# One decode step: the last row of wo in two column halves, the output in two PSUM banks, the tail of w_out on 12 lanes

## The chip, the cores and the metric

The kernel runs on one core of a Trainium2 chip. The core has a matrix engine (TensorE, PE in the profile, with its weight loads as PEld), a vector engine (VectorE, DVE), a scalar engine (ScalarE, ACT), GpSimd (POOL) and a sequencer that issues most of the DMAs (SyncE, SP), and 16 DMA engines that move data between device memory (HBM) and on-chip memory (SBUF). [...]

The metric is device time in microseconds (us) for one execution of the whole program. Three runs of the kernel before gave 661.06, 661.14 and 661.30 us; the median is 661.14.

## The reference

One token for each of 4 sequences is normalized (LayerNorm, D = 640) and goes through two branches in parallel, whose results are added to the input:

```python
xn = _layernorm(x)
return x + _A_ref(xn, k_cache, v_cache, wq, wo) + _B_ref(xn, w_in, w_sp, b_sp, w_out)

# A: attention over a cache, 32 heads of 128, 4096 positions, batch 4, bf16
q = (x @ wq) split into heads
scores = einsum('bhqd,bhkd->bhqk', q, k) * 128 ** -0.5
o = einsum('bhqk,bhkd->bhqd', softmax(scores), v)
return o (as rows of 4096) @ wo                  # wo: 4096 x 640

# B: gated MLP
z = gelu(einsum('bsd,df->bsf', x, w_in))         # w_in: 640 x 1728
z1, z2 = z[..., :864], layernorm(z[..., 864:])
g = w_sp * z2 + b_sp                             # 1 x 1 spatial weight
return einsum('bsf,fd->bsd', z1 * g, w_out)      # w_out: 864 x 640
```

K and V together are 268 MB of bf16, and each element is used once.

## The kernel before, in words

**Tiles.** The 32 heads are taken in four groups of eight. One step `i` of the main loop (16 in all) does one group of heads for one sequence; its K tile and its V tile are 8 MB each, 128 partitions by 64 KB, and each is loaded by one DMA. K has two slots in SBUF; V has one. wq first sits in a K slot, w_in and w_out first sit in the V slot (`w_sb`, lines 106 to 126), and wo takes the V slot at the end.

**Start.** SP issues w_out's first 768 rows (line 109), wq (114), w_in (121), the last 96 rows of w_out (line 123, four DMAs), and then the first K tile. These last 96 rows lie on `TL` = 16 lanes (partitions) with `TK` = 6 rows each, and each of the four DMAs fills 4 of the lanes (`TE`), every fourth one. The query projection (line 271) computes 4096 columns in two halves in two PSUM tiles of pool `ps_pv`; ACT copies each half (line 278), PE transposes it. The second K tile is issued when wq has been used.

**gMLP.** Branch B runs between the query projection and the loop (`gmlp`, lines 309 to 421). For the last 96 rows, `TK` small matmuls (line 408) gather the activations of every `TK`-th column on `TL` lanes (`ye_ps`, copied to `yE`). Then `NFC` = 12 calls of `add_out` add everything to the output: six on 128 lanes, six on 16 lanes. The first V tile may only be issued (line 145) when these matmuls have read w_sb.

**Loop.** DVE multiplies the K tile by the query in place (449), folds it in half (463); PE sums by matmuls with an identity (475), DVE finishes the row sums (486). Then maximum, exponential (542), the weights spread to each head's own lanes (553), and 64 matmuls per tile with V (`weighted`, 568) into one PSUM tile `pv`. ACT copies `pv` to `e` (`take`, 578) and PE picks each head's own rows out of `e` into `o_ps` (`diag`, 591). The order of PE, DVE, ACT and SP in the loop is the order in which the code is written.

**wo.** After the last step but one has used its V tile, SP issues wo (`load_wo`, line 154) into the V slot: the first half of the heads (`g` = 0) in one DMA, the second (`g` = 1) in three, rows 0 to 10, 11 to 14 and 15 of each partition (`WO_CUTS`). The last V tile is loaded before it, into a K slot.

**End.** After the last V tile: 64 matmuls, copy, `diag`, normalization and spreading (619, 628), turning (643), and the projection `group_proj` with 16 rows of four matmuls each (`add_out`, line 216), one for each quarter of the 640 columns. A quarter `q` lies in PSUM on partitions 32q to 32q + 3, all four in one bank, the tile `out_ps`. The four matmuls of row 15 stop the accumulation. Then ACT copies the first two quarters to `res` and DVE the last two (735), and each half is stored by a DMA of its own, the first from ACT's queue and the second from SP's (739).

Of the kernel before, what the change touches and what calls it, by code (L numbers as in the profile page):

```python
# [9 lines left out]
FP32 = mybir.dt.float32  # L10
# [7 lines left out]
def kernel(  # L18
# [14 lines left out]
    nc = tc.nc  # L33
    P = nc.NUM_PARTITIONS
    Bsz, Sq, D = A_x.shape
    _, H, S, Dh = A_k_cache.shape
    HD = A_wq.shape[1]
    F = B_w_in.shape[1]
    Fh = F // 2
# [18 lines left out]
    GW = P // CG  # L58
    ROWS = HT * Bsz
    NG = 2  # L60
    HP = HG // NG
    WH = NG * HT
    WL = P // WH
    WJ = WH * Dh // P
    WW = 2
    WR = NG * ROWS
    NFF = Fh // P
    TL = 16
    TK = (Fh - NFF * P) // TL
    TE = 4  # L70
    NFC = NFF + TK
    F0 = NFF * P
    TF = TL * TK
    NZ = NFF + 1
    assert F0 + TF == Fh and TF <= P
    NQ = 4
    NO = D // NQ
# [8 lines left out]
    pmp = ctx.enter_context(tc.tile_pool(name="pmp", bufs=1))  # L86
    PSUM = bass.MemoryType.PSUM
    ps_s = ctx.enter_context(tc.tile_pool(name="ps_s", bufs=1, space=PSUM))
    ps_pv = ctx.enter_context(tc.tile_pool(name="ps_pv", bufs=2, space=PSUM))
    ps_m = ctx.enter_context(tc.tile_pool(name="ps_m", bufs=2, space=PSUM))  # L90
    ps_o = ctx.enter_context(tc.tile_pool(name="ps_o", bufs=1, space=PSUM))
    ps_out = ctx.enter_context(tc.tile_pool(name="ps_out", bufs=1, space=PSUM))
# [4 lines left out]
    def v_slot(name):  # L97
        return vp.tile([P, SLOT], BF16, tag="v", name=name)
# [9 lines left out]
    w_out_sb = w_sb[:, DC * F : DC * F + NFC * D].rearrange("p (k n) -> p k n", k=NFC)  # L108
    nc.sync.dma_start(
        out=w_out_sb[:, 0:NFF, :], in_=B_w_out[0 : NFF * P].rearrange("(p k) n -> p k n", k=NFF)  # L110
# [10 lines left out]
    nc.sync.dma_start(out=w_in_sb, in_=B_w_in.rearrange("(p c) n -> p c n", c=DC))  # L121
    for l in range(TL // TE):
        nc.sync.dma_start(
            out=w_out_sb[:TL, NFF:NFC, :].rearrange("(e l) k n -> e l (k n)", e=TE)[:, l],
            in_=B_w_out[F0:Fh].rearrange("(e l k) n -> e l (k n)", e=TE, k=TK)[:, l],
        )

    def kv_view(cache, i):
# [8 lines left out]
    def load_k(i):  # L137
        t = k_slot("k_nat")
        nc.sync.dma_start(out=t[:], in_=kv_view(A_k_cache, i))
        k_tiles[i] = t[:].rearrange("p (c d) -> p c d", d=Dh)  # L140

    def load_v(i, t):
        cuts = V_CUTS if i == NT - 1 else (0, NC)
        for c0, c1 in zip(cuts, cuts[1:]):
            nc.sync.dma_start(
                out=t[:, c0 * Dh : c1 * Dh], in_=kv_view(A_v_cache, i)[:, c0 * Dh : c1 * Dh]
            )
        v_tiles[i] = t[:].rearrange("p (c d) -> p c d", d=Dh)

    wo_v = A_wo.rearrange("(g p j) n -> g p j n", p=P, j=WJ)  # L150
    wo_t = []
    WO_CUTS = ((0, WJ), (0, 11, 15, WJ))

    def load_wo():
        t = v_slot("wo")[:, 0 : HP * WJ * D].rearrange("p (g j n) -> p g j n", g=HP, n=D)
        wo_t.append(t)
        for g in range(HP):
            for j0, j1 in zip(WO_CUTS[g], WO_CUTS[g][1:]):
                nc.sync.dma_start(out=t[:, g, j0:j1, :], in_=wo_v[g][:, j0:j1, :])

    load_k(0)

# [19 lines left out]
    for i in range(NSTAT):  # L182
# [5 lines left out]
        out=rstd[:], in_=mv[:, 1:2], func=ACT.Sqrt, bias=eps_tile[:Bsz], scale=1.0  # L188
# [3 lines left out]
        out=xn_bf,  # L192
# [9 lines left out]
    for c in range(DC):  # L202
        nc.tensor.transpose(
            out=xnT_ps[:, c, :], in_=xn_v[:, c, :], identity=ident[:Bsz, :Bsz]
# [3 lines left out]
        out=xnT_r[:], in_=xnT_ps[:, :, :, None].to_broadcast([P, DC, Bsz, REP])  # L208
    )
    xnT = xnT_r[:, :, :, 0]  # L210

    out_ps = ps_out.tile([P, NO], FP32)

    def add_out(lhsT, rhs, start=False, stop=False):
        for q in range(NQ):
            nc.tensor.matmul(  # L216
                out=out_ps[GW * q : GW * q + lhsT.shape[1], :],
                lhsT=lhsT,
                rhs=rhs[:, q * NO : (q + 1) * NO],
                start=start,  # L220
                stop=stop,
            )
# [6 lines left out]
        out=own[:], in_=ident_f[:].rearrange("p (h l) -> p h l", h=HT), axis=AX.X, op=ALU.add  # L229
# [4 lines left out]
        out=pick[:, :, GW - HT : GW],  # L234
        in_=ident_f[:].rearrange("p (j h c) -> p c h j", c=CB, h=HT),
# [5 lines left out]
        out=row_head_f[:],  # L241
        in_=ident_f[:WR, :WR].rearrange("p (g b h) -> p g h b", g=NG, h=HT),
# [5 lines left out]
        out=row_head[:],  # L248
        in_=row_head_f[:].rearrange("p g h -> p (g h)")[:, :, None].to_broadcast([WR, WH, WL]),
# [3 lines left out]
        out=row_batch_f[:],  # L253
        in_=ident_f[:WR, :WR].rearrange("p (g b h) -> p b g h", g=NG, h=HT),
# [12 lines left out]
    for t in range(2):  # L267
        for c in range(DC):
            for j in range(CG):
                n = CG * t + j  # L270
                nc.tensor.matmul(  # L271
                    out=q_ps[t][GW * j : GW * (j + 1), :],
                    lhsT=xnT_r[:, c].rearrange("p b r -> p (b r)"),
# [5 lines left out]
    for t in range(2):  # L279
        qT_ps = ps_m.tile([P, HQ, CG, Bsz, REP], BF16, tag="m", name="qT_ps")  # L280
        for n in range(HQ):
            nc.tensor.transpose(  # L282
                out=qT_ps[:, n].rearrange("p j b r -> p (j b r)"),
                in_=q_rows[:, t, n * Dh : (n + 1) * Dh],
# [3 lines left out]
            out=qT[:, CG * HQ * t : CG * HQ * (t + 1), :].rearrange(  # L288
                "p (j n) b -> p n j b", n=HQ
            ),  # L290
            in_=qT_ps[:, :, :, :, 0],
# [17 lines left out]
    def gmlp():  # L309
# [95 lines left out]
        nc.vector.tensor_tensor(out=yT[:], in0=gz[:, 0, :, :], in1=sq, op=ALU.mult)  # L405
        ye_ps = ps_m.tile([TL, TK, Bsz], FP32, tag="m", name="ye_ps")
        for k in range(TK):
# [6 lines left out]
            )  # L414
        yE = work.tile([TL, TK, Bsz], BF16, name="yE")
        nc.scalar.copy(out=yE[:], in_=ye_ps[:])
# [10 lines left out]
    def stage_q(i):  # L427
        hg, b = divmod(i, Bsz)
        q_l = small.tile([P, HT, LN], BF16, name="q_l", bufs=1)
        nc.scalar.copy(  # L430
            out=q_l[:],
            in_=qT[:, HT * hg : HT * (hg + 1), b : b + 1].to_broadcast([P, HT, LN]),
        )
        qb_ps = ps_m.tile([P, Dh], FP32, tag="m", name="qbc_ps")
        nc.tensor.matmul(  # L435
            out=qb_ps[:],
            lhsT=q_l[:].rearrange("p h l -> p (h l)"),
            rhs=ident[:],
            start=True,
            stop=True,  # L440
        )
        qbcs[i] = small.tile([P, Dh], BF16, name="qbc")
        nc.scalar.copy(out=qbcs[i][:], in_=qb_ps[:])  # L443
# [217 lines left out]
    def at(i, fn, *args):  # L661
        if 0 <= i < NT:
            fn(i, *args)
# [10 lines left out]
    with tc.manual_schedule(engines={E.PE, E.DVE, E.Activation, E.SP}):  # L674
        stage_q(0)
        gmlp()
        load_v(0, v_slot("v_nat"))
        for i in range(NT):
            product(i, 0)
            at(i - 1, row_sums, 1)  # L680
            at(i - 1, lane_max)
            at(i - 1, turn_max)
            at(i - 1, head_max)
            at(i - 1, spread_max)
            fold(i, 0)
            joined(i - 2, group_rows)
            sums(i, 0)
            joined(i - 2, group_turn)
            at(i - 1, bias)
            at(i - 1, exps)  # L690
            at(i + 1, stage_q)
            at(i - 1, own_heads)
            at(i - 1, weighted)
            if i == 0:
                pass
            elif i < NT - 1:
                load_v(i, v_slot("v_nat"))
            else:
                load_wo()
            at(i - 1, take)  # L700
            product(i, 1)
            row_sums(i, 0)
            fold(i, 1)
            at(i - 1, diag)
            group(i - 1, group_den)
            sums(i, 1)
            if i + 2 < NT:
                load_k(i + 2)
            elif i + 2 == NT:
                load_v(NT - 1, k_slot("v_last"))  # L710
        L = NT - 1
        row_sums(L, 1)
        lane_max(L)
        joined(L - 1, group_rows)
        turn_max(L)
        head_max(L)
        spread_max(L)
        bias(L)
        exps(L)
        own_heads(L)  # L720
        for c0, c1 in zip(V_CUTS, V_CUTS[1:]):
            weighted(L, c0, c1)
        take(L)
        group_den(HG - 1)
        diag(L)
        group_rows(HP - 1)
        group_proj(0)
        group_turn(HP - 1)
        group_proj(HP - 1)

        res = small.tile([Bsz, D], BF16, tag="s_sb", name="res", bufs=1)
        halves = ((nc.scalar.copy, nc.scalar), (nc.vector.tensor_copy, nc.sync))
        for h, (copy, _) in enumerate(halves):
            for q in range(NQ // 2 * h, NQ // 2 * (h + 1)):
                copy(out=res[:, q * NO : (q + 1) * NO], in_=out_ps[GW * q : GW * q + Bsz])
        out_v = out.flatten_outer_dims()
        for h, (_, queue) in enumerate(halves):
            cols = slice(D // 2 * h, D // 2 * (h + 1))
            queue.dma_start(out=out_v[:, cols], in_=res[:, cols])


# [28 lines left out]
```

## Time and profile before

| what | value |
|---|---|
| median of three runs | 661.14 us |
| the profiled execution | 661.22 us |
| its span on the core | 659.4 us |
| bytes read from HBM | 282.24 MB, 428 GB/s over the span |
| share of 16 DMA engines busy, SP's queue | 99.0% |
| DVE busy | 492.3 us (75%) |
| PE busy | 298.0 us (45%) |
| mean granted TensorE clock | 0.713 |
| output copies, each | 0.28 us on ACT, 0.32 us on DVE |

A line of the timeline gives start, time from the first start to the last end, engine, line of the kernel, operation, the tiles written and read, their shapes, and in brackets how long the engine sat idle before and what ended that. A line of the chain of waits gives start, duration, engine and tile of what the end of the program depended on. "SPq" and "ACTq" are issues of DMAs by SP and ACT. The profile also keeps a record of each DMA packet, with its start, size and duration, and of each semaphore's rise. Its clock starts at the first instruction, and all times in the text count from there.

### The profile page before, as it was taken

Reading aid. Unit: us, or ns where it says so; the run is one execution under the profiler, and the core shown is the slowest. Engines: PE = TensorE matmul, PEld = TensorE weight load, DVE = VectorE, ACT = ScalarE, POOL = GpSimd, SP = SyncE. Lnnn points to the kernel's source line nnn. Section 1 sums busy time; section 2 is a strip of 40 time slices with the busy share of each in tenths; the row PEclk is TensorE's granted clock in tenths of the full one; section 3 lists DMA queues with packets and bytes.
Section 4 is the critical chain, followed back from the end, with each engine's and each line's share of the span. In section 5 each row is a group of like instructions: output and inputs, shape, how many; then the busy total and the mean of one; then the engine's idle time right before and its main releaser. Section 6 shows DMA issues by size and latency. Waiting matters only on the chain.

```text
span 659.4 us, 4721 instructions
## 1 busy us (share of the span) xinstructions
PE 298.0 (45%) x2099; PEld 129.0 (20%) x2099; DVE 492.3 (75%) x224; ACT 34.7 (5%) x95; POOL 2.1 (0%) x15
## 2 busy tenths in 40 slices
PE   0513464535426253542626344362734616273656
PEld 0301121212112021210202112120311202121223
DVE  1249999959597795959879569986959699695861
ACT  0300000000000000000000000000000000000000
POOL 1000000000000000000000000000000000000000
PEclk9756676876858687585868757786685758668698
DMA  9999999999999999999999999999999999999996
GB/s 378 445 441 445 406 442 438 426 445 426 429 441 430 429 442 426 441 426 421 445 437 434 441 422 425 445 430 437 434 430 433 446 417 434 429 445 438 437 399 296
DMA packets 5696, 282.55 MB, mean 429 GB/s; under 512 B 656, under 2 KB 796, under 8 KB 1068
## 3 DMA queue, kind: packets, MB, share of 16 engines
q1 hardware_dynamic: 5656, 282.24, 99.0%
q8 instruction: 16, 0.26, 0.1%
q14 instruction: 4, 0.03, 0.0%
q10 hardware_dynamic: 20, 0.01, 0.0%
HBM read 282.24 MB, written 0.01 MB: 428 GB/s over the span
## 4 chain that ended last, share of the span: by engine, by line
DMA 49%; DVE 40%; PE 8%; issue 2%; ACT 1%; SPq 0%; DVEq 0%
DMA k_nat<-in_A_k_cache_dram 42%; DVE k_nat L449 24%; DVE k_nat L463 12%; DMA v_last<-in_A_v_cache_dram 6%; PE s_ps L475 6%; DVE s_sb L486 3%; PE pv L568 1%; ACT p L542 1%; DMA w_sb<-in_B_w_out_dram 1%; DVE m L495 1%; PE mT L500 0%; DVE nm L505 0%; PE out_ps L216 0%; DVE wide L628 0%; PE o_ps L591 0%
## 5 line engine op out<-in xcount | busy, mean ns | idle before, releaser
L449 DVE TENSOR_TENSOR k_nat<-k_nat,qbc 128x16384 bf16<-128x16384 bf16 x32 | 278.0, 8688 | 96.3 <-DMA k_nat<-in_A_k_cache_dram 96.3
L475 PE MATMUL s_ps<-k_nat,ident 128*128 128x512 bf16 x528 | 186.7, 532 | 137.7 <-DVE k_nat L463 137.7
L463 DVE TENSOR_TENSOR k_nat<-k_nat 128x8192 bf16<-128x8192 bf16 x31 | 136.7, 4410 | 0.0
L475 PEld LDWEIGHTS <-ident 128*128 128x128 bf16 x528 | 65.9, 130 | 248.0 <-DVE k_nat L463 121.6
L500 PE MATMUL mT<-ident_f,m 128*1 128x128 f32 x16 | 5.9, 366 | 157.9 <-DVE m L495 157.9
L568 PE MATMUL pv<-v_nat,pm 128*32 128x512 bf16 x960 | 56.2, 388 | 0.8 <-DVE pm L553 0.8
L486 DVE TENSOR_REDUCE s_sb<-s_ps 128x128 f32<-128x1024 f32 x32 | 39.0, 1218 | 3.8 <-PE s_ps L475 3.7
L568 PEld LDWEIGHTS <-pm 128*32 128x32 bf16 x1024 | 27.5, 101 | 36.1 <-issue 10.8
L500 PEld LDWEIGHTS mT<-ident_f,m 128*1 128x1 f32 x16 | 1.3, 79 | 165.7 <-DVE m L495 154.5
L553 DVE TENSOR_TENSOR pm<-p,own_c 128x2048 bf16<-128x2048 bf16 x16 | 19.6, 1226 | 15.7 <-ACT p L542 15.7
L542 ACT ACTIVATE p<-s_sb,nb 128x256 bf16<-128x256 f32 x16 | 8.1, 508 | 388.5 <-DVE nb_h L524 388.5
L591 PE MATMUL o_ps<-e,pick 128*32 128x128 f32 x128 | 17.0, 276 | 11.2 <-ACT e L578 11.2
L591 PEld LDWEIGHTS o_ps<-e,pick 128*32 128x32 f32 x128 | 12.7, 109 | 18.7 <-ACT e L578 18.7
L578 ACT COPY e<-pv 128x512 f32<-128x512 f32 x16 | 9.4, 586 | 70.9 <-PE pv L568 61.3
L287 DVE COPY qT<-qT_ps 128x64 bf16<-128x64 bf16 x2 | 0.4, 224 | 15.5 <-PE qT_ps L282 15.5
L516 PE MATMUL nb_ps<-nm,ones_row 1*128 1x8 f32 x32 | 9.2, 359 | 6.0 <-DVE nm L505 6.0
L505 DVE TENSOR_REDUCE nm<-mT 1x8 f32<-1x128 f32 x16 | 4.5, 279 | 7.5 <-PE mT L500 7.5
L516 PEld LDWEIGHTS nb_ps<-nm,ones_row 1*128 1x128 f32 x32 | 7.7, 299 | 10.6 <-DVE nm L505 9.9
L271 PE MATMUL q_ps<-wq,xnT_r 128*32 128x512 bf16 x40 | 4.2, 603 | 11.2 <-DMA wq<-in_A_wq_dram 11.2
L443 ACT CAST qbc<-qbc_ps 128x128 bf16<-128x128 f32 x16 | 4.3, 267 | 94.6 <-PE qbc_ps L435 94.6
L568 PE MATMUL pv<-v_last,pm 128*32 128x512 bf16 x64 | 6.3, 577 | 4.1 <-DMA v_last<-in_A_v_cache_dram 4.1
L608 PE MATMUL den<-ones_col,acc_h 128*32 128x1 f32 x8 | 1.0, 194 | 15.5 <-DVE acc_h L601 15.5
(93 smaller groups left out, 72.6 us busy)
## 6 DMA issues: line engine op xcount, KB each, us to landing
wq<-in_A_wq_dram SPq DMA_DIRECT2D x1, 5120.0 KB, 16.3
wo<-in_A_wo_dram SPq DMA_DIRECT2D x1, 2560.0 KB
w_sb<-in_B_w_in_dram SPq DMA_DIRECT2D x1, 2160.0 KB, 21.0
wo<-in_A_wo_dram SPq DMA_DIRECT2D x1, 1760.0 KB
w_sb<-in_B_w_out_dram SPq DMA_DIRECT2D x1, 960.0 KB
wo<-in_A_wo_dram SPq DMA_DIRECT2D x1, 640.0 KB, 24.6
k_nat<-in_A_k_cache_dram SPq DMA_DIRECT2D x16, 39.2
v_nat<-in_A_v_cache_dram SPq DMA_DIRECT2D x15, 33.3
```

Source lines behind the costliest of these rows:

```text
L449: nc.vector.tensor_tensor(out=part(i, u), in0=part(i, u), in1=qbcs[i][:, None, :].to_broadcast([P, UC, Dh]), op=ALU.mult,)
L463: nc.vector.tensor_tensor(out=t[:, :, 0:HD2], in0=t[:, :, 0:HD2], in1=t[:, :, HD2:Dh], op=ALU.add)
L475: nc.tensor.matmul(out=sums_ps[i][:, c : c + SC], lhsT=ident[:], rhs=t[:, c : c + SC, g * RW : (g + 1) * RW], start=(g == 0), stop=(g == n ...
L486: nc.vector.tensor_reduce(out=scores[i][:, u * UC : (u + 1) * UC], in_=sums_ps[i][:], axis=AX.X, op=ALU.add,)
L495: nc.vector.tensor_reduce(out=m1[:], in_=scores[i][:], axis=AX.X, op=ALU.max)
L500: nc.tensor.transpose(out=mT[:], in_=maxes[i][:], identity=ident_f[:])
L516: nc.tensor.matmul(out=nb_ps[:], lhsT=ones_row[:], rhs=maxes[i][:], start=True, stop=True)
L542: nc.scalar.activation(out=probs[i][:], in_=scores.pop(i)[:], func=ACT.Exp, bias=maxes.pop(i)[:], scale=scale_qk, accum_out=accs[hg][:, b ...
L553: nc.vector.tensor_tensor(out=pm[:], in0=probs.pop(i)[:] .rearrange("p (n c) -> p n c", c=CB)[:, :, None, :] .to_broadcast([P, NB, HT, CB] ...
L568: nc.tensor.matmul(out=pvs[i][j * GW : (j + 1) * GW, :], lhsT=pm[:, n, :, :].rearrange("p h c -> p (h c)"), rhs=v_nat[:, n * CB : (n + 1) ...
L578: nc.scalar.copy(out=es[i][:], in_=pvs.pop(i)[:].rearrange("p (c d) -> p c d", d=Dh))
L591: nc.tensor.matmul(out=o_ps[hg // NG][own_rows(hg), :], lhsT=pick[:, c, GW - HT - HT * b : 2 * GW - HT - HT * b], rhs=e[:, c, :], start=(b ...
```

## The change

There are four edits.

1. `TL` becomes 12, so `TK` becomes 8: the last 96 rows of w_out lie on 12 lanes by eight rows, loaded by three DMAs of four neighbouring lanes each. `NFC` becomes 14.
2. Pool `ps_pv` has one buffer instead of two. The freed bank goes to the output.
3. Row 15 of wo's second half is loaded by two DMAs, one for each half of the 640 columns.
4. The output has two PSUM tiles in two banks, one for each half of the columns. In each half ACT copies one quarter and DVE the other. The second half is stored from ACT's queue, the first from SP's.

```diff
-    TL = 16
+    TL = 12
...
-    ps_pv = ctx.enter_context(tc.tile_pool(name="ps_pv", bufs=2, space=PSUM))
+    ps_pv = ctx.enter_context(tc.tile_pool(name="ps_pv", bufs=1, space=PSUM))
...
-            out=w_out_sb[:TL, NFF:NFC, :].rearrange("(e l) k n -> e l (k n)", e=TE)[:, l],
-            in_=B_w_out[F0:Fh].rearrange("(e l k) n -> e l (k n)", e=TE, k=TK)[:, l],
+            out=w_out_sb[:TL, NFF:NFC, :].rearrange("(l e) k n -> l e (k n)", e=TE)[l],
+            in_=B_w_out[F0:Fh].rearrange("(l e k) n -> l e (k n)", e=TE, k=TK)[l],
...
-    WO_CUTS = ((0, WJ), (0, 11, 15, WJ))
+    WO_CUTS = ((0, WJ), (0, 11, 15))
+    NH = 2
+    QH = NQ // NH
+    DH = D // NH
...
+        for h in range(NH):
+            cols = slice(DH * h, DH * (h + 1))
+            nc.sync.dma_start(
+                out=t[:, HP - 1, WJ - 1, cols], in_=wo_v[HP - 1][:, WJ - 1, cols]
+            )
...
-    out_ps = ps_out.tile([P, NO], FP32)
+    out_ps = [ps_out.tile([P, NO], FP32, name=f"out_ps{h}") for h in range(NH)]
...
-                out=out_ps[GW * q : GW * q + lhsT.shape[1], :],
+                out=out_ps[q // QH][GW * q : GW * q + lhsT.shape[1], :],
...
-        halves = ((nc.scalar.copy, nc.scalar), (nc.vector.tensor_copy, nc.sync))
-        for h, (copy, _) in enumerate(halves):
-            for q in range(NQ // 2 * h, NQ // 2 * (h + 1)):
-                copy(out=res[:, q * NO : (q + 1) * NO], in_=out_ps[GW * q : GW * q + Bsz])
+        for h in range(NH):
+            for q, copy in zip(range(QH * h, QH * (h + 1)), (nc.scalar.copy, nc.vector.tensor_copy)):
+                copy(
+                    out=res[:, q * NO : (q + 1) * NO], in_=out_ps[h][GW * q : GW * q + Bsz]
+                )
         out_v = out.flatten_outer_dims()
-        for h, (_, queue) in enumerate(halves):
-            cols = slice(D // 2 * h, D // 2 * (h + 1))
+        for h, queue in ((1, nc.scalar), (0, nc.sync)):
+            cols = slice(DH * h, DH * (h + 1))
             queue.dma_start(out=out_v[:, cols], in_=res[:, cols])
```

## The prediction

> **What bounds the kernel now.** I read the page first, part 3 before part 1: one DMA queue is busy for 99% of the span on all 16 engines, and no compute engine comes near that.
>
> ```profile
> PE 298.0 (45%) x2099; PEld 129.0 (20%) x2099; DVE 492.3 (75%) x224; ACT 34.7 (5%) x95; POOL 2.1 (0%) x15
> ...
> q1 hardware_dynamic: 5656, 282.24, 99.0%
> ```
>
> The reader is to see that the DMA engines have no room: 282 MB pass at about 430 GB/s whatever the other engines do, so an edit counts only where it changes the bytes, the moment at which the queue starts, a moment at which it runs dry, or what follows the last landing. Two places of the change lie elsewhere, at the start. I therefore read the timeline of the first 45 us, to see what covers them:
>
> ```profile
> 2.17 3.90 SPq L123 DMA_DIRECT2D w_sb<-in_B_w_out_dram  x4
> 6.12 16.05 SPq L139 DMA_DIRECT2D k_nat<-in_A_k_cache_dram  x2
> 17.58 4.21 PE L271 MATMUL q_ps<-wq,xnT_r 128*32 128x512 bf16 x40 [11.23 <-DMA wq<-in_A_wq_dram]
> 19.95 0.59 ACT L278 CAST q_rows<-q_ps 128x512 bf16<-128x512 f32 x1 [14.92 <-PE q_ps L271]
> 34.66 0.96 PE L216 MATMUL out_ps<-w_sb,yE 16*4 16x160 bf16 x24
> 35.67 0.33 SPq L145 DMA_DIRECT2D v_nat<-in_A_v_cache_dram  x1
> 43.30 8.69 DVE L449 TENSOR_TENSOR k_nat<-k_nat,qbc 128x16384 bf16<-128x16384 bf16 x1 [9.75 <-DMA k_nat<-in_A_k_cache_dram]
> ```
>
> Here the thing to see is distance. The first K tile lands at 43.3; the second was issued at 21.8 and the first V at 35.67. A K tile takes about 19.5 us at 430 GB/s, so the queue has work until about 62 without that V.
>
> The end I read in three views: the chain of waits from 643 us on, the wo line by itself, and the timeline of the last 4 us.
>
> ```profile
> 644.09 6.27 PE pv L568 x64
> ...
> 654.75 0.22 ACT oT L651
> 654.97 0.04 issue
> 655.01 1.54 PE out_ps L216 x64
> 656.55 0.31 DVE res L735
> 656.86 0.35 DVEq L765
> ```
>
> ```profile
> L159 SPq DMA_DIRECT2D wo<-in_A_wo_dram x4: 328/433/435, 630.4 to 631.7; - x4
> ...
> DMA to landing us min/median/max: 24.5/24.5/24.6
> ```
>
> ```profile
> 655.01 1.43 PE L216 MATMUL out_ps<-wo,oT 128*4 128x160 bf16 x64 [0.30 <-ACT oT L651]
> 656.53 0.59 ACT L735 CAST res<-out_ps 4x160 bf16<-4x160 f32 x2 [1.57 <-PE out_ps L216]
> 656.54 0.67 DVE L735 CAST res<-out_ps 4x160 bf16<-4x160 f32 x2 [2.24 <-PE out_ps L216]
> 657.15 0.27 ACTq L739 DMA_DIRECT2D out_dram<-res  x1
> 657.24 0.30 SPq L739 DMA_DIRECT2D out_dram<-res  x1
> ```
>
> The chain credits the arithmetic behind the last V, but the wo line says that a second path ends at the same moment: the last row of wo is issued at 631.7 and lands 24.5 us later, at 656.2 (656.16 in the trace's semaphore records). The last four of the 64 projection matmuls need that row. By the records matmuls come in fours every 0.069 us; row 14's four start at 656.03, the last four at 656.21 instead of 656.10. So they wait 0.1 us for the row. Then come 0.32 us from the last matmul to the copies, two copies on each engine, and two stores. The stores' semaphores rise at 658.34 (ACT's) and 658.52 (SP's); SP's is last, and the span closes 0.83 us behind it.
>
> **The change, part by part.**
>
> *Tail rows of w_out, 12 lanes by eight.* Removed: one of four issues at the start (0.6 us of SP). The bytes are the same: 4 transfers of 4 packets of 7,680 B become 3 of 4 packets of 10,240 B. In the packet records the old 16 run in four rows of four, 0.29 us each, so four engines carry 1.16 us more than the others; the new load per engine, worked out at the same bytes per ns, is 3 x 0.39 = 1.16 us. Queue: SP reaches the first K tile up to 0.6 us earlier, and its packets start at 22.0 in any case, behind wq and w_in. Cost 0. PE gets 2 more gather matmuls (about 0.06 us each here) and 8 more projections (24 in 0.96 us, so 0.32 us): 0.45 us more before the first V may overwrite w_sb. Cover: the K tile in flight until about 62, against a V issued at 35.67. How the new form spreads over engines is not in the trace. From below, spread over all 16, four engines are relieved of 0.87 us; from above, all 122,880 B on one engine are 16 x 0.29 = 4.64 us there. I take four engines, since a transfer of four rows went to four engines before. [...]
>
> *One pv buffer.* The only place where two pv tiles live at once is the query projection: its second half must now wait for the copy of the first. The row is that copy, 0.59 us, plus some 0.2 us of hand-over: 0.6 to 0.9 us on the query path, which SP (second K tile, 21.8) and gMLP wait behind. Together with the 0.45 above that is about 1.2 us, covered by the same queue: the second K tile is needed on the queue at about 42, the V at about 62. If that cover were gone, the whole 1.2 us would show. In the loop, PE itself runs the o_ps matmuls on the copied tile before it reaches the next pv, so the only buffer is free by then: 0.
>
> *Last row in two halves.* SP issues five transfers instead of four (0.43 us more, at 632, with 20 us to spare before the queue reaches them). The packets are 128 of 1,280 B before and 256 of 640 B after. The records price them: 1,280 B took 55 ns, 640 B (the output's own) 29 to 32 ns. Each engine has 8 rows: 440 ns become 2 x 244 plus one more semaphore write of 9 ns. The first half lands 0.19 us sooner (655.98), the second 0.06 us later (656.22). For the extra transfer the ends are 0, if the small packets pipeline fully, and 1.28 us, a store's time from issue to landing (657.24 to 658.52), if the second half starts afresh behind the first. I take 0.06, because packet prices are the nearest row, and the last two transfers of wo land only 0.4 us apart (655.8 and 656.2, for a 160 KB row), so a start in series isn't paid today. [...]
>
> *Two banks, copies shared, stores by halves.* The first half's two matmuls now wait for nothing and start at 656.10; copies can follow 0.32 us later, at 656.42: ACT (0.28 each, 0.30 apart) and DVE (0.32, 0.34 apart). The second half's matmuls start at 656.27, its copies may start at 656.59, and the engines are free at 656.72 and 656.76. So its copies run to 657.00 and 657.09, against 657.21 now. Both engines read one bank at once already (656.53 and 656.54), so I charge nothing for that. SP stores the first half at about 656.8, well ahead of the end. ACT's store now waits for DVE too; nothing stands behind it on its queue, and an extra semaphore wait on SP takes 0.03 us in this trace. It issues at about 657.15, as now, and lands as now, at 658.34. What goes is the SP landing at 658.52: gain 0.18, less 0.03.
>
> *Sum.* 0 + 0 + 0 - 0.15 us; the 0.06 of the later half is inside the copy times. The profiled execution took 661.22 (span 659.4), 0.08 above the median of 661.14. So 661.07 there, and 661.0 at the median. The range of this case alone: -0.4 (if the last landing does not move and the shorter copies show in full) to +0.25 (the 0.4 us between landings, less the gain), so 660.7 to 661.4.
>
> **Rivals.**
>
> *The change buys nothing at the end.* If ACT's store is slower than SP's once it waits for both engines (SP took 1.28 us from issue to landing, ACT 1.19), the 0.15 is eaten: 661.1 to 661.3. For it: only 0.1 us separates the stores. Against: nothing in the row above.
>
> *The throttle.* The granted clock was 0.50 from 642.6 to 649.5 and 1.00 after that. The landing of wo and the arithmetic now end together, so slower arithmetic goes straight to the end. One more half-speed step of 3.4 us (the steps of the clock records) stretches the end of pv and half of o_ps: +1.15, 662.1. If it lasted past 656, the last o_ps (+0.9), t_ps (+0.2) and projection would double too; 24 projections took 0.96 us at 0.50, so 64 take 2.56 instead of 1.28: about +2.4 in all, 663.4. From there on it is slower. For: PE's work at the start moves by a microsecond. Against: the last 100 us of PE's work are the same, and three runs lie within 0.24 us.
>
> *The tail transfer on one engine.* This is the case on the other side of the forecast with a clear price. By the records the engines write their last-row semaphores between 652.6 and 655.8. An engine that ended at 652.6 and got 4.64 us would end at 657.2, 1.4 us behind today's last: 662.5; a late one would give 664 or more. It decides once one engine gets more than 3.2 us beyond its share. Against: the four rows of packets.
>
> *The second half pays a start of its own* of 1.28 us: it lands at 655.98 + 0.24 + 1.28 = 657.50, its copies run 657.87 to 658.21, the store issues near 658.3 and lands at 659.5, 1.0 us behind today's last landing: 662.1. Against: the 0.4 us between landings.
>
> *Faster by over 1.3 us* needs both paths shorter, an earlier landing (tail spread over 16 engines, up to 0.87) and faster pv (clock 1.00 there): I see neither coming, 659.7 if both came.
>
> **How the numbers follow.** The forecast has 0.69, no gain at the end 0.08, one more half-speed step 0.03, a start of its own 0.03: 0.83 within 0.2% (1.32 us, about what a measurement of this kernel can tell from no change). Slower: throttle to the end 0.05, tail on one engine 0.06, so 0.11. Faster 0.06. The range takes the first four cases, 660.5 to 662.2, with 0.2 us below the likeliest case's own low end for the spread of runs.
>
> **What would show it.** Right: three transfers of 40 KB and two of 80 KB among the issues; the second q_ps half starting about 0.7 us after the first ends; first V issued near 37 and first K product still at 43.3; SP's store near 0.3 us ahead of ACT's; two copies on each engine, the first starting near 0.1 us earlier relative to the last matmul; DMA share unchanged. Wrong: the last wo landing later than 656.5 on that scale, a granted clock of 0.50 after 650, a first K product past 44, or ACT's store landing later than 1.25 us after its issue.

## The result: 0.19% slower, and the loss starts in the first 25 us

Over 16 runs of each, the changed kernel has a median of 662.33 us (661.67 to 663.41) and the kernel before 661.08 (660.87 to 661.37). The ratio is 1.0019, with a 95% interval of 1.0011 to 1.0027. The forecast was 661.0, in a range of 660.5 to 662.2: the sign is wrong, and the median lies just above the range. The profiled execution is the slowest of the 16 (663.41, span 661.6). So its end shows more loss than the median has; where the extra comes from is taken up further down.

The page of the changed kernel, the line of the large queue:

```profile
q1 hardware_dynamic: 5792, 282.24, 98.9%
```

The bytes are the same and the queue is as busy as before (99.0%), over a span that is 2.2 us longer. The same packets have taken longer, then, or stood still. The timeline of the start says since when:

```profile
2.17 1.34 SPq L123 DMA_DIRECT2D w_sb<-in_B_w_out_dram  x3
5.55 17.79 SPq L139 DMA_DIRECT2D k_nat<-in_A_k_cache_dram  x2
...
20.62 2.32 PE L279 MATMUL q_ps<-wq,xnT_r 128*32 128x512 bf16 x20 [0.68 <-ACT q_rows L286]
...
36.39 0.33 SPq L145 DMA_DIRECT2D v_nat<-in_A_v_cache_dram  x1
44.74 8.69 DVE L457 TENSOR_TENSOR k_nat<-k_nat,qbc 128x16384 bf16<-128x16384 bf16 x1 [10.79 <-DMA k_nat<-in_A_k_cache_dram]
```

SP is 0.6 us earlier at the first K tile, PE pays 0.68 us for the single pv buffer, and the first V is issued at 36.39: all as the prediction had it. But DVE starts on the first K tile at 44.74 instead of 43.30. It waits for the DMA: the tile's semaphore rises sixteen times, the last at 44.72 instead of 43.27, and DVE starts 0.02 us after that (before 0.03). So the tile lands 1.4 us later.

At the end, the chain of waits now runs through wo:

```profile
633.20 25.02 DMA wo<-in_A_wo_dram
...
658.27 0.55 PE out_ps L224 x18
...
658.84 0.32 DVE res L742
```

and the timeline shows the new order of copies and stores:

```profile
658.27 0.66 PE L224 MATMUL out_ps<-wo,oT 128*4 128x160 bf16 x20 [0.19 <-DMA wo<-in_A_wo_dram]
658.84 0.67 DVE L742 CAST res<-out_ps 4x160 bf16<-4x160 f32 x2 [2.41 <-PE out_ps L224]
658.86 0.59 ACT L742 CAST res<-out_ps 4x160 bf16<-4x160 f32 x2 [1.77 <-PE out_ps L224]
659.26 0.29 SPq L748 DMA_DIRECT2D out_dram<-res  x1
659.59 0.27 ACTq L748 DMA_DIRECT2D out_dram<-res  x1
```

Here the reader sees an end that works as forecast. SP's store goes out 0.33 us ahead of ACT's, and from the last landing of wo (658.65) to the end of the span it takes 2.98 us, against 3.19 before. The landing itself is 2.5 us later than before.

The packet records show what changed at 22 us. (They don't name the engine; packets that follow each other without a gap are taken here as those of one engine.) The 16 old tail packets of w_out took 291 ns each, 4.66 us in all. The 12 new ones take 385, 385, 385, 385, 693, 1056, 1179, 1239, 595, 548, 791 and 812 ns, in order of time: 8.45 us. They again run as four rows, here of three packets each, so four engines carry them. And they are not alone. On the other 12 engines the first packet of the first K tile, 64 KB, takes 3.01 to 3.03 us instead of 2.42. The four engines of the tail start on the tile at 23.7 to 24.7, before at 23.2 to 23.4. Followed packet by packet they end their parts of it at 43.1 to 44.2 (before 42.6 to 42.7), and eleven of the other twelve at 41.9 to 42.3 (before 41.4 to 41.7).

### The profile page after: what moved, and what is told of

Its sections match the earlier page's. It is cut to its first block, busy times and chain, and to the rows that moved or that the text cites. A ratio compares the mean times of both kernels' runs of the same rounds, so it can differ in the third digit from the quotient of the medians.

```text
span 661.6 us, 4741 instructions
## 1 busy us (share of the span) xinstructions
PE 293.5 (44%) x2109; PEld 127.7 (19%) x2109; DVE 492.2 (74%) x224; ACT 34.7 (5%) x95; POOL 2.1 (0%) x15
## 3 DMA queue, kind: packets, MB, share of 16 engines
q1 hardware_dynamic: 5792, 282.24, 98.9%
## 4 chain that ended last, share of the span: by engine, by line
DMA 51%; DVE 37%; PE 9%; issue 2%; ACT 1%; SPq 0%; DVEq 0%
DMA k_nat<-in_A_k_cache_dram 47%; DVE k_nat L457 22%; DVE k_nat L471 11%; PE s_ps L483 8%; DMA wo<-in_A_wo_dram 4%; DVE s_sb L494 3%; DMA w_sb<-in_B_w_out_dram 1%; ACT p L550 1%; PE pv L576 1%; DVE m L503 1%; PE mT L508 0%; DVE nm L513 0%; DVE pm L561 0%; SPq L162 0%; PE nb_ps L524 0%
## 5 line engine op out<-in xcount | busy, mean ns | idle before, releaser
L483 PE MATMUL s_ps<-k_nat,ident 128*128 128x512 bf16 x528 | 181.5, 520 | 142.4 <-DVE k_nat L471 142.4
```

The costliest lines, as they stand in the source:

```text
L483: nc.tensor.matmul(out=sums_ps[i][:, c : c + SC], lhsT=ident[:], rhs=t[:, c : c + SC, g * RW : (g + 1) * RW], start=(g == 0), stop=(g == n ...
```

## The experiments

Two theories stood at first. *The lanes*: four engines that write neighbouring lanes at once hold each other up. *The size*: larger packets in fewer transfers are slow. A third, *the end*, had the loss in the halves, the banks or the single buffer. All times are medians beside runs of the kernel before on the same chip (661.10, 661.20, 661.13 and 661.17 in the four groups of runs).

### The old tail in the changed kernel

```diff
-    TL = 12
+    TL = 16
...
-            out=w_out_sb[:TL, NFF:NFC, :].rearrange("(l e) k n -> l e (k n)", e=TE)[l],
-            in_=B_w_out[F0:Fh].rearrange("(l e k) n -> l e (k n)", e=TE, k=TK)[l],
+            out=w_out_sb[:TL, NFF:NFC, :].rearrange("(e l) k n -> e l (k n)", e=TE)[:, l],
+            in_=B_w_out[F0:Fh].rearrange("(e l k) n -> e l (k n)", e=TE, k=TK)[:, l],
```

> The changed kernel with the tail rows of w_out as before (16 lanes by six, four transfers to every fourth lane); one pv buffer, halves and banks stay. If the new tail is the whole loss (both theories on the tail, neighbouring lanes or larger packets): the tail's 16 packets at 0.29 us each again, last landing of wo near 656.2, and 660.9 to 661.0, that is 0.1 to 0.2 below before. If the halves, the banks or the single pv buffer cost it: 662.3 still.

Measured: 661.02 us, ratio 0.9998 (0.9989 to 1.0007). All 16 tail packets are back at 291 ns, and wo lands at 656.07. The timeline:

```profile
43.26 8.69 DVE L457 TENSOR_TENSOR k_nat<-k_nat,qbc 128x16384 bf16<-128x16384 bf16 x1 [10.05 <-DMA k_nat<-in_A_k_cache_dram]
```

The whole loss is gone with the new tail, so the theory of the end falls. The 0.1 us below before is what the forecast has for the other edits, but it is inside the interval.

### The new tail alone

```diff
-    TL = 16
+    TL = 12
...
-            out=w_out_sb[:TL, NFF:NFC, :].rearrange("(e l) k n -> e l (k n)", e=TE)[:, l],
-            in_=B_w_out[F0:Fh].rearrange("(e l k) n -> e l (k n)", e=TE, k=TK)[:, l],
+            out=w_out_sb[:TL, NFF:NFC, :].rearrange("(l e) k n -> l e (k n)", e=TE)[l],
+            in_=B_w_out[F0:Fh].rearrange("(l e k) n -> l e (k n)", e=TE, k=TK)[l],
```

> The kernel before with the new tail alone (12 lanes by eight, three transfers of four neighbouring lanes). Both theories on the tail: 662.3 to 662.6, tail packets of 0.4 to 1.2 us instead of 0.39. If the end of the kernel costs it: 661.1.

Measured: 662.17 us, ratio 1.0015 (1.0006 to 1.0023), tail packets of 385 to 1,255 ns, first K packets of the other engines 3.48 to 3.49 us:

```profile
44.93 8.69 DVE L449 TENSOR_TENSOR k_nat<-k_nat,qbc 128x16384 bf16<-128x16384 bf16 x1 [12.17 <-DMA k_nat<-in_A_k_cache_dram]
```

A loss of 1.07 us from this edit by itself.

### Neighbouring lanes with the old packets

Only the two view lines of the diff above; `TL` stays 16.

> The kernel before with 16 lanes by six as it was, but each of the four transfers fills four neighbouring lanes instead of every fourth. Same packets (16 of 7,680 B), same bytes per engine, same matmuls. Theory of the lanes (four engines that write neighbouring lanes at once hold each other up): packets well over 0.29 us, up to about 1 us, and 662.0 to 662.6. Theory of the size (10,240 B in three transfers is what is slow): 0.29 us each and 661.1.

Measured: 661.89 us, ratio 1.0010 (1.0001 to 1.0019). Packets of the old size take 291 to 829 ns (7.10 us in all), other engines' first K packets 3.28 to 3.29 us. So the size isn't needed for the loss.

### Every third lane with the new packets

```diff
-    TL = 16
+    TL = 12
```

> The kernel before with 12 lanes by eight (10,240 B, three transfers), but each transfer fills every third lane (0,3,6,9 and so on), so that at most two of its four lanes lie in the same group of four. Theory of the lanes: less hold-up than with neighbours, packets of 0.39 to 0.8 us, 661.2 to 661.8. Theory of the size: as with neighbours, 662.3 or more.

Measured, in four runs: 669.26 us, ratio 1.0122 (1.0108 to 1.0136). Neither theory had that, and the timeline shows that the run tested something else as well:

```profile
2.56 0.45 SPq L139 DMA_DIRECT2D k_nat<-in_A_k_cache_dram  x1
22.71 1.98 SPq L123 DMA_DIRECT2D w_sb<-in_B_w_out_dram  x3
```

With this view SP waits 19.7 us with the tail transfers, for w_in's landing, and they are queued behind the first K tile. PE then starts gMLP at 43.6 instead of 23.8, DVE, whose last step of gMLP starts at 53.13, reaches the first K product at 53.23, and the third K tile is issued at 85.98. In stretches of five microseconds:

```profile
80.00:85.00 5.00, 4.50 (x13) 1.71 (x14) 5.00 (x2) 0.00 (x0) 0.00 (x0) 0.58 0.00 0
85.00:90.00 5.00, 0.95 (x5) 0.22 (x3) 5.00 (x2) 0.00 (x0) 0.00 (x0) 1.00 0.62 223
```

The last two columns are the share and the GB/s of the DMA engines: a dry queue for about 6 us. As a test of lanes its time says nothing. Its packets say a little: 10,240 B took 385 ns in nine of twelve cases and at most 551.

### Lanes and source apart

In the third experiment both sides of the transfer became contiguous. The next two change one side each.

```diff
-            out=w_out_sb[:TL, NFF:NFC, :].rearrange("(e l) k n -> e l (k n)", e=TE)[:, l],
+            out=w_out_sb[:TL, NFF:NFC, :].rearrange("(l e) k n -> l e (k n)", e=TE)[l],
```

> The kernel before, its four tail transfers to four neighbouring lanes each, but read from four rows that lie apart in HBM, as before; so blocks of w_out sit on other lanes than their activations and the tail's part of the output is not the reference's. Theory of the lanes (writing neighbouring lanes from four engines): as with neighbours on both sides, tail packets up to 0.8 us, first K packets of the other engines over 3 us, 661.7 to 662.1. Theory of the source (four engines reading one contiguous stretch of HBM): 0.29 us each, 661.1.

Measured: 661.98 us, ratio 1.0013 (1.0004 to 1.0022); tail packets up to 744 ns (7.58 us in all), other engines' first K packets 3.40 to 3.41 us.

```diff
-            in_=B_w_out[F0:Fh].rearrange("(e l k) n -> e l (k n)", e=TE, k=TK)[:, l],
+            in_=B_w_out[F0:Fh].rearrange("(l e k) n -> l e (k n)", e=TE, k=TK)[l],
```

> The reverse: tail transfers to every fourth lane as before, each read from one contiguous 30 KB of HBM; again the tail's part of the output is not the reference's. Theory of the lanes: 0.29 us each and 661.1. Theory of the source: packets up to 0.8 us and 661.7 to 662.1.

Measured: 661.09 us, ratio 0.9997 (0.9988 to 1.0006); 291 ns for each tail packet. The timelines, lanes first, source second:

```profile
44.65 8.69 DVE L449 TENSOR_TENSOR k_nat<-k_nat,qbc 128x16384 bf16<-128x16384 bf16 x1 [12.03 <-DMA k_nat<-in_A_k_cache_dram]
```

```profile
43.35 8.69 DVE L449 TENSOR_TENSOR k_nat<-k_nat,qbc 128x16384 bf16<-128x16384 bf16 x1 [9.63 <-DMA k_nat<-in_A_k_cache_dram]
```

It is the lanes that are written, not the rows that are read.

### How near is near?

Every second lane instead of every fourth:

```diff
-            out=w_out_sb[:TL, NFF:NFC, :].rearrange("(e l) k n -> e l (k n)", e=TE)[:, l],
-            in_=B_w_out[F0:Fh].rearrange("(e l k) n -> e l (k n)", e=TE, k=TK)[:, l],
+            out=w_out_sb[:TL, NFF:NFC, :].rearrange("(a e c) k n -> a c e (k n)", a=2, e=TE)[l // 2, l % 2],
+            in_=B_w_out[F0:Fh].rearrange("(a e c k) n -> a c e (k n)", a=2, e=TE, k=TK)[l // 2, l % 2],
```

> The kernel before with each tail transfer to every second lane (0,2,4,6; 1,3,5,7; 8,10,12,14; 9,11,13,15): two of its four lanes in each group of four. If the hold-up comes from how many engines write into one group of four lanes: about half of what four do, tail packets between 0.29 and 0.6 us, 661.3 to 661.6. If only direct neighbours (lane n and n+1) hold each other up: 0.29 us and 661.1 to 661.2.

Measured: 661.59 us, ratio 1.0006 (0.9997 to 1.0015); tail packets 291 to 545 ns (5.94 us in all), other engines' first K packets 2.79 to 2.80 us. Two in a group of four do about half of what four do; the time alone would not show it, the packets do.

Lanes 32 apart:

```diff
-            out=w_out_sb[:TL, NFF:NFC, :].rearrange("(e l) k n -> e l (k n)", e=TE)[:, l],
+            out=w_out_sb[:, NFF:NFC, :].rearrange("(e a r) k n -> a r e (k n)", e=TE, r=4)[l, 0],
...
-        for k in range(NFC):
+        for k in range(NFF):
```

> The kernel before with each tail transfer to four lanes 32 apart (0,32,64,96; 4,36,68,100 and so on); the matmuls of the tail rows are left out, so the output lacks their part (24 matmuls, about 1 us of PE at the start, covered). Theory of nearness (lanes of one group of four): none of the four is near another, 0.29 us each and 661.0 to 661.1. [...]

Measured: 661.75 us, ratio 1.0009 (1.0000 to 1.0018); tail packets 291 to 514 ns (5.99 us), other engines' first K packets 2.96 to 3.21 us. Far apart, and held up as much as every second lane: nearness falls as well. Tail totals are 7.10 to 9.10 us in the four profiles with four neighbouring lanes, 5.94 with every second lane, 5.99 with every 32nd and 4.66 with every fourth: the lanes that are written together decide, and by what rule isn't shown. While the tail is written, the other engines write the K tile, which covers all 128 lanes. Which of these lanes they write at that moment isn't in the records, so the last experiment doesn't keep an effect of theirs apart from that of the tail's own lanes.

### Other ways to lay out the tail

On the changed kernel's end, 32 lanes by three rows, eight lanes at distance four in each transfer; and one transfer to 96 lanes of one row.

```diff
-    TL = 12
+    TL = 32
...
-    TE = 4
+    TE = 8
```

> The changed kernel's end with the tail on 32 lanes by three rows, four transfers of eight lanes, every fourth lane. Eight engines carry 0.58 us each instead of four with 1.16. Theory of the lanes: no packet held up, 660.6 to 661.1; near the low end if the four loaded engines are among the last to finish, near the high end if they are not. Theory of the size: no statement.

```diff
-    TL = 12
+    TL = 96
...
+    nc.sync.dma_start(
+        out=w_out_sb[:TL, NFF:NFC, :],
+        in_=B_w_out[F0:Fh].rearrange("(l k) n -> l k n", k=TK),
+    )
```

> The changed kernel's end with the tail as one transfer on 96 lanes, one row each: all 16 engines carry six packets of 1,280 B, 0.33 us, and their lanes lie six apart. Theory of the lanes: little hold-up; 660.3 if the loaded engines were the last to finish, 661.3 (0.33 later than with four) if they were not. Fewer matmuls in gMLP change nothing.

(Both take the old views, or none, in place of the changed ones.) Measured: 661.47 us (1.0005, 0.9996 to 1.0013) and 661.44 us (1.0007, 0.9998 to 1.0015). The 32 packets take 149 ns each and the 96 take 55 ns each, so none of them is held up. With 96 lanes, though, the first K packet of every engine takes 2.48 to 2.53 us instead of 2.42. The last landing of wo moves to 656.62 and 656.42, from 656.16. That would fit if engines without tail rows in the kernel before are among the last to finish, and the four that carry them have room for it; the records can't confirm it, as they don't name the engines, and both intervals include no change. The first of the two misses its range by 0.4 us, and this is the likely reason. Nor do the records show the share that was expected for 96 lanes, six rows on each engine and six lanes apart.

### The two parts of the new end

Row 15 in halves alone (`WO_CUTS` and the loop of the change, one bank), and banks, copies and stores alone, with row 15 whole:

> The kernel before with row 15 of wo in two column halves and nothing else (one output bank, copies and stores as before). The copies wait for the last matmul of all, so the second half's later landing counts in full: 0.06 us later by the packet prices, 661.1 to 661.2; time from the last landing of wo to the end of the span 3.2 us as before.

> The kernel before with one pv buffer, two output banks, copies by both engines in each half and stores by halves; row 15 of wo in one transfer. Both halves' matmuls then start together at the landing; SP's store is early, ACT's comes at its old time: 0.1 to 0.15 us less from the last landing to the end of the span (3.05 instead of 3.2), 660.9 to 661.0, not to be told from 661.1 by the medians alone.

Measured: 661.25 us (1.0002, 0.9993 to 1.0010) and 661.00 us (0.9999, 0.9990 to 1.0008). The medians lie on the forecast sides of 661.13, but can't be told from it. The profiles are finer: from the last landing of wo to the end of the span it takes 3.16 us with halves alone and 3.13 with banks alone. With both it is 2.98 to 3.11 in four kernels (mean 3.05), and 3.18 to 3.37 in ten kernels with the old end (mean 3.22). So the new end with both parts takes about 0.17 us less there. One part alone takes 0.06 or 0.09 us less than that mean, in one profile each, while the ten differ by 0.19 among themselves: how the gain divides isn't shown.

### A second hold-up: the third K tile

In the profiled execution of the changed kernel packets are slow once more: five of the third K tile, from 80.6 us on, take 3.75 to 4.24 us. No profile of an experiment above has one of over 3 us there, apart from the one with the dry queue. SP issues this tile when PE has summed the rows of the first one. Before:

```profile
70.57 6.30 PE L475 MATMUL s_ps<-k_nat,ident 128*128 128x512 bf16 x16 [7.52 <-DVE k_nat L463]
76.91 0.33 SPq L139 DMA_DIRECT2D k_nat<-in_A_k_cache_dram  x1
```

In the changed kernel:

```profile
72.02 6.47 PE L483 MATMUL s_ps<-k_nat,ident 128*128 128x512 bf16 x16 [9.04 <-DVE k_nat L471]
78.52 0.33 SPq L139 DMA_DIRECT2D k_nat<-in_A_k_cache_dram  x1
```

With the new tail alone:

```profile
72.21 5.26 PE L475 MATMUL s_ps<-k_nat,ident 128*128 128x512 bf16 x16 [8.56 <-DVE k_nat L463]
77.51 0.33 SPq L139 DMA_DIRECT2D k_nat<-in_A_k_cache_dram  x1
```

By the packet records the first engines have run out of V packets at 80.5 in the changed kernel and at 80.0 before: a margin of 2.0 us instead of 3.1. The late first tile takes from this margin, but not alone. With the new tail by itself the first tile is even later (44.93), and yet the margin is 3.35 us (the engines run out at 80.86) and no packet of the third tile is slow. What differs is PE's clock: the granted clock rises from 0.50 to 1.00 at 77.8 in the changed kernel and at 75.6 with the new tail alone, so the 16 matmuls take 6.47 and 5.26 us. Two more kernels with a late first tile lie in order: a rise at 76.1 (lanes alone) leaves 3.37 us, one at 77.2 (16 neighbouring lanes) 2.54.

To see whether the margin matters, idle matmuls delay the issue in the kernel before (4 and 9 of them):

```diff
+        for x in range(4 if (i, u) == (0, 1) else 0):
+            nc.tensor.matmul(
+                out=sums_ps[i][:, 0:SC], lhsT=ident[:], rhs=t[:, 0:SC, 0:RW], start=True, stop=True
+            )
         for c in range(0, UC, SC):
```

> The kernel before with 4 more matmuls (their result is overwritten) ahead of the second half of the first row sums, at half clock 0.39 us each: the third K tile is issued 1.6 us later, near 78.5, as in the profiled run of the change. If that margin of some 1.5 us ahead of the first idle engine is too small: packets over 3 us at 80 to 81 us and 661.5 to 662.2. If the second hold-up is chance: 661.1 and no such packet.

> The same with 9 more matmuls, 3.5 us: issue near 80.4, after the first engines have run out. By either theory some engines are dry: packets over 3 us, 0.5 to 2 us of loss, 661.6 to 663.1. If even this costs nothing, the queue's margin isn't what the profile seems to say.

Measured: 661.96 us (1.0011, 1.0002 to 1.0020) and 662.47 us (1.0018, 1.0009 to 1.0027). The delays in the profiled executions are smaller than planned, since part of the matmuls ran at full clock (from 75.0 and 76.0 us on). The longer one:

```profile
78.82 0.33 SPq L139 DMA_DIRECT2D k_nat<-in_A_k_cache_dram  x1
```

Its first engines run out at 80.0, 1.2 us after the issue, and packets of the third K tile take up to 3.47 us. The next V is issued at 94.98 (before at 95.06), so only this one issue has moved. With four matmuls the issue was at 77.36 (margin 2.4 us), packets took up to 2.83 us, and that execution took 661.34; the eleven runs spread from 661.03 to 662.47.

All profiles but the one with the dry queue can be set side by side. With a margin of 3.06 us or more (nine kernels) the longest packet that starts between 79.7 and 85 us takes 2.63 us at most; at 2.9 us (two) it takes 2.74; at 2.5 and 2.4 us 2.95 and 2.83; at 2.0 and 1.2 us 4.24 and 3.47. So in these profiles a third K tile issued 2.0 or 1.2 us before the first engine ran dry had slow packets. In the changed kernel some engines also stood without a packet for a moment: from 80.58 to 81.84 us its records have at times only 13 to 15 packets under way at once, where those of the kernel before have 16 throughout. The two delays cost 0.8 and 1.3 us at the median. The margins of the runs without a profile are unknown, and engines may have run dry for longer in some of them: the profiled execution of the longer delay took 661.85 and was the fastest of its eleven. The cost is shown for the kernel before. That it is also what happened in the profiled execution of the changed kernel, and in which of its other runs, is argued from the same margin.

## Why the prediction was wrong, point by point

- **The bound: right.** DMA busy at 98.9 to 99.0%, so only what touches the queue counts. The change touched it.
- **The tail rows at cost 0: wrong, and it decides.** The step that failed is "the new load per engine, worked out at the same bytes per ns, is 3 x 0.39 = 1.16 us". Measured was 8.45 us on four engines instead of 4.66, so about 0.95 us more on each, and 0.6 us (0.9 to 1.1 in the three experiments with four neighbouring lanes) on each of the other twelve. That edit alone cost 1.07 us, where the prediction had "Cost 0". The bounds of the step (all 16 engines, one engine) varied how many engines carry the bytes. Four it was; the price came from where the four write. The row that should have warned is the old view itself: "every fourth one" of the lanes is a choice, and the diff undoes it. The step asked which engines read the rows, and never which lanes they write at once.
- **The rival "tail transfer on one engine" gave a time near the measured one (662.5) for a wrong reason:** no engine got extra bytes.
- **One pv buffer: right.** 0.68 us on PE (forecast 0.6 to 0.9), first V at 36.39 (near 37), and the kernel with the old tail shows no loss from it.
- **The cover at the start: only half examined.** The second K tile and the first V had 20 us of cover, as said. The third K tile, 40 us later, has 3.1 us, and the prediction did not look at it. In the profiled execution a first K tile that landed 1.4 us late, with the queue's own work only 0.5 us later, left 2.0.
- **The halves and the banks: right.** Expected gain 0.15 us; 0.17 from the profiles, SP's store 0.33 us ahead (forecast 0.3). The two halves of row 15 landed 0.19 us apart (658.46 and 658.65), so the second paid no start of its own. The medians can't tell the gain from nothing (0.9998, 0.9989 to 1.0007).
- **The throttle: right for the end, overlooked in the middle.** The granted clock was 0.50 until 651.2 and 1.00 after that. So the sign "a granted clock of 0.50 after 650" came too, but only because everything was 2 us later; the 64 matmuls with V took 5.93 us instead of 6.27. At 72 to 78 us, where the prediction did not look, the clock decides how much of the third K tile's margin is left.
- **The chance of 0.83 within 0.2% came true by luck.** The ratio is 1.0019, but by none of the four cases that the 0.83 was made of.
- **What the text named as a sign of being wrong came:** "a first K product past 44" (44.74) and a last landing later than 656.5 (658.65).

## What to carry to other kernels

When a diff changes how a small DMA is spread over lanes, ask which lanes are written at the same moment, not only how many bytes each engine gets: a 120 KB load at the wrong lanes held up the twelve engines without a part in it for 0.6 to 1.1 us, and the four that carried it for longer. In this kernel, bound by its DMA queue, that pause was not made up (1.07 us for this edit alone), so 0.04% of the bytes decided the sign of the whole change. And cover must be examined at every issue that follows a delayed one, up to the one with the smallest margin.

## What was not expected of the hardware

- **Engines without a part in the tail paused too.** The other twelve engines' first K packets are longer by nearly the same amount within a run (3.48 to 3.49 us on all twelve with the new tail alone, 2.79 to 2.80 with every second lane; only with lanes 32 apart they differ, 2.96 to 3.21), though they carry no packet of the tail. Why is open.
- **The first transfer to four neighbouring lanes was not held up:** its four packets took 385 ns (291 for the smaller ones) in each of the four profiles, the least that any packet of their size took, and of the tail's packets only those behind it took longer.
- **Packets that reached an engine with little to spare were slow:** 64 KB took up to 3.47 us instead of 2.42 when the tile was issued 1.2 us before the engine's earlier work ended, and up to 4.24 with 2.0 us. Why is open, and the margin alone doesn't set how slow they are.
